# Block-causal attention and two FFN layers: the low words' shift on ScalarE, their scaling within VectorE's product, and two early weight halves instead of four

## The chip, the cores and the metric

The kernel runs on one core of one Trainium2 chip. The metric is the device time of one execution in microseconds (us). Before the change three runs took 1007.52, 1007.89 and 1008.43 us; their median is 1007.89 us.

Five engines work in parallel, each on its own queue in order: TensorE (PE in the profile; its weight loads are PEld), VectorE (DVE), ScalarE (ACT), GpSimd (POOL) and SyncE (SP, which here only issues transfers).

## The reference, cut to what matters

The input is q, k, v of shape (4, 8, 576, 64) in float32 and two pairs of weights of 512x2048 and 2048x512.

```python
# block-causal attention: a query sees the keys of its own block of 64 and of earlier blocks
scores = q @ k.T / 8, masked;  attn = softmax(scores);  attn_out = attn @ v
x = attn_out as 2304 tokens x 512
h = x @ w_in;   x = relu(h)**2 @ w_out          # first FFN layer  ("layer 0")
h = x @ w2_in;  y = (h * cos(h)) @ w2_out       # second FFN layer ("layer 1")
```

## The kernel before, in words

**Attention.** Batch and head give 32 attentions, taken two at a time: 16 pairs, 0 to 15. For each pair there are nine blocks of 64 queries. PE makes the scores of a block (`add_scores`), DVE their maximum, ACT the exponentials with their sums; GpSimd scales the probabilities by the reciprocal of the sums (L431), PE transposes them (L452), ACT and DVE split them into a high and a low part (L457, L460), GpSimd splits the values in the same way (L486, L492), PE multiplies (L517), ACT moves one half across the partitions (L528) and DVE adds and writes the result into `xall` (L531, "join"). The order of all this on each engine is not written out: a planner (`Plan`, L52 on) puts every step into an order by walking through the program with an assumed cost for each step. Among steps that could start at the same moment it takes the one with the lowest rank, and the rank is the step's number in the program plus the entry of its kind in the table `RANK`.

**Weights.** The weights of both layers come as float64. A "half" (class `Half`) is one 128x512 chunk of `w_in` or of `w_out`, 512 KB, loaded into a `raw` tile (four buffers), in which each weight is a low and a high 32-bit word. Its steps turn the two words into two float32 tiles, a high part and a remainder, that PE then multiplies: on DVE `shift` (L205), `mask` (L212), `join` (L223), `sign` (L235), `power` (L241) and `low` (L265); on ACT `rebias` (L218), `fraction` (L229) and `high` (L256, a copy). `low` multiplies the scaled low words by each weight's power of two. Layer 0 has 32 halves and layer 1 another 32.

**Early halves.** Four halves of layer 0 are converted by the planner inside attention (`add_half`), not before the first score step of the last pair (the key `late`); their `high` runs on GpSimd (L259). Their raw words are loaded early.

**Layers.** Each layer goes over blocks of up to 512 tokens, and each block over 16 chunks of 128 hidden features, which gives one *step* per chunk. In a step PE makes `hidden` of this chunk (12 matmuls, L619) and `output` of the chunk three steps back (12 matmuls, L683); in between, ACT and DVE turn the hidden values into a high part (L631) and a low part `gs` (L634). At each step `convert` is called as often as the table `PACE` says: twice per step in block 0, which is how the other 28 halves of layer 0 are made while block 0 runs. One call of `convert` finishes the half that the call before began and begins the next. In layer 0's last block the halves of layer 1 follow, 1.75 calls per step and 0.75 in the block after it. At the end of a block the next block's tokens are split as well (class `Cut`, L315 on ACT and L318 on DVE), into one set of `xs` tiles.

**PSUM.** Attention uses eight banks: six handed round by the planner (`ps0` to `ps5`) and two for the widest block. The layers use the same eight, `h0` to `h3` on the places of `ps0` to `ps3`. So the first `hidden` (into `h1`) can't be written until the last reader of `ps1` in attention is done.

Of the kernel before, what the change touches and what calls it, by code (L numbers as in the profile page):

```python
# [24 lines left out]


RANK = {
    "load": -388.7,
    "k scale": -506.7,
    "scores": 0.2,  # L30
    "maximum": -16.0,
    "exponential": 485.3,
    "guard": -148.0,
    "invert": -12.1,
    "scale": -145.6,
    "turn": 13.1,
    "turned high": -90.7,
    "turned low": -1.1,
    "value load": -78.8,
    "value high": -109.4,  # L40
    "value low": 28.0,
    "weighted": 21.6,
    "move": 1000,
    "join": 34.2,
    "keep": 67.5,
    "add": 125.4,
    "zeros": -32.1,
    "weights": 181.2,
    "cut": 1000000.0,
}  # L50

# [1 line left out]
class Plan:  # L53
# [12 lines left out]
        self.steps, self.wrote, self.readers = [], {}, {}  # L66
        self.held, self.taken = {}, {}

    def add(self, engine, cost, at, emit, reads=(), writes=(), holds=0, frees=None):
        n, after, (kind, rank) = len(self.steps), set(), at  # L70
        rank += RANK[kind]
        for key in reads:
            after.add(self.wrote.get(key))
            self.readers.setdefault(key, []).append(n)
        for key in writes:
            after.add(self.wrote.get(key))
            after.update(self.readers.pop(key, ()))
            self.wrote[key] = n
        self.steps.append((engine, cost, rank, emit, after - {None, n}, holds, frees))
        return n  # L80

    def emit(self):
        waits = [len(step[4]) for step in self.steps]
        follow = [[] for _ in self.steps]
        for n, step in enumerate(self.steps):
            for m in step[4]:
                follow[m].append(n)
        able, clock = {}, {}
        start = [0.0] * len(self.steps)
        for n, step in enumerate(self.steps):  # L90
            clock[step[0]] = 0.0
            able.setdefault(step[0], [])
            if not waits[n]:
                able[step[0]].append(n)
        free = [(0.0, b) for b in range(len(self.banks))]
        held = self.held
        for _ in self.steps:
            best = None
            for engine, mine in able.items():
                times = {}  # L100
                for n in mine:
                    holds = self.steps[n][5]
                    if holds <= len(free):
                        times[n] = max(start[n], clock[engine], free[holds - 1][0] if holds else 0.0)
                if times:
                    t = min(times.values())
                    n = min((n for n in times if times[n] <= t), key=lambda n: (self.steps[n][2], n))
                    if best is None or t < best[0]:
                        best = (t, n)
            t, n = best  # L110
            engine, cost, _, emit, _, holds, frees = self.steps[n]
            able[engine].remove(n)
            clock[engine] = t + cost
            if holds:
                self.taken[n] = [free.pop(0)[1] for _ in range(holds)]
                held[n] = [self.banks[b] for b in self.taken[n]]
            key = n if holds else frees
            emit(*(held[key] if key is not None else []))
            if frees is not None:
                free = sorted(free + [(t + cost + 0.37, b) for b in self.taken[frees]])  # L120
            for m in follow[n]:
                other = self.steps[m][0]
                lag = self.SIGNAL.get((engine, other), 0.06 if engine == other else 0.15)
# [7 lines left out]
def tile_block_causal_attention__then__two_ffn(  # L131
# [38 lines left out]
    nc.vector.memset(new_bias, -7.0 * 2.0**30)  # L170

    WARM = 15
    EARLY = 4
    NA = 5
    w_a = ctx.enter_context(tc.tile_pool(name="w_a", bufs=NA))
    xs_p = ctx.enter_context(tc.tile_pool(name="xs", bufs=1))
# [16 lines left out]
    class Half:  # L193
# [8 lines left out]
            nc.sync.dma_start(out=self.raw, in_=packed[self.key[0]][self.key[1], self.h])  # L202

        def shift(self):
            nc.vector.tensor_scalar(  # L205
                out=self.low_word, in0=self.low_word, scalar1=9, scalar2=None,
                op0=ALU.logical_shift_right,
            )

        def mask(self):  # L210
# [11 lines left out]
        def join(self):  # L222
            nc.vector.scalar_tensor_tensor(  # L223
                out=self.low_word, in0=self.high_word, scalar=23, in1=self.low_word,
                op0=ALU.logical_shift_left, op1=ALU.bitwise_or,
            )

        def fraction(self):
            nc.scalar.activation(  # L229
                out=self.low_word.bitcast(F32), in_=self.low_word.bitcast(U32), func=AF.Copy,  # L230
                scale=2.0**-43,
            )

        def sign(self):
# [20 lines left out]
        def high(self):  # L255
            nc.scalar.copy(out=self.room()[:, 0], in_=self.bits.bitcast(F32))  # L256

        def high_beside(self):
            nc.gpsimd.tensor_scalar(  # L259
                out=self.room()[:, 0], in0=self.bits.bitcast(F32), scalar1=1.0, scalar2=0.0,  # L260
                op0=ALU.mult, op1=ALU.add,
            )

        def low(self):
            nc.vector.tensor_tensor(  # L265
                out=self.room()[:, 1], in0=self.low_word.bitcast(F32),
                in1=self.high_word.bitcast(F32), op=ALU.mult,
            )

    later = []  # L270

    def flush():
        while later:
            later.pop()()

    def convert():

        old = new = None
        flush()
        if begun:  # L280
            (layer, c), h = begun[0].key, begun[0].h
            if layer == 1 and c >= freed[h]:
# [3 lines left out]
        if loaded:  # L286
            new = loaded.pop(0)
            begun.append(new)
            new.shift()
        if old:  # L290
            old.power()
            old.high()
        if new:
            new.mask()
            new.rebias()
        if old:
            old.low()
        if new:
            new.join()
            later.append(new.fraction)  # L300
        if loads:
            loaded.append(Half(*loads.pop()))
            loaded[-1].load()
# [21 lines left out]
    def attention():  # L325
        with ExitStack() as actx:
# [224 lines left out]
            def add_half(n):  # L551
                x = Half(*loads.pop())
                raw, high, bits = f"raw{n % 4}", f"high{n % 4}", f"bits{n % 2}"
                rank = ("weights", n)
                late = f"S{NPAIR - 1}.0"
                plan.add("D", 2.0, rank, x.load, writes=[raw, high])
                plan.add("V", 0.34, rank, x.shift, [late], [raw])
                plan.add("V", 0.34, rank, x.mask, [high, late], [bits])
                plan.add("A", 0.61, rank, x.rebias, writes=[bits])
                plan.add("V", 0.6, rank, x.join, [high], [raw])  # L560
                plan.add("A", 0.52, rank, x.fraction, writes=[raw])
                plan.add("V", 0.6, rank, x.sign, [high], [bits])
                plan.add("V", 0.34, rank, x.power, [bits], [high])
                plan.add("G", 0.67, rank, x.high_beside, [bits])
                plan.add("V", 0.6, rank, x.low, [raw, high])

            make_identity(nc, ident)

# [31 lines left out]
    def layers():  # L600
# [112 lines left out]
                t0 += n  # L713
        last = max(i for i, b in enumerate(blocks) if b[0] == 0)
        steps = [(i, c) for i in range(len(blocks)) for c in range(KF)]
        PACE = {0: 2, last: 1.75, last + 1: 0.75}
        owed = 0.0
        gss = {}
        xs = first
# [1 line left out]
        for step in range(len(steps) + LAG):  # L721
# [10 lines left out]
            for a, z in zip_longest(begin, [None] + end):  # L732
                for f in (a, z):
                    if f:
                        f()
                flush()
# [68 lines left out]
```

## Time and profile before

| | us |
|---|---|
| median of three runs | 1007.89 |
| the profiled execution | 1008.09 |
| its span, first to last instruction | 1006.3 |
| PE busy | 981.6 (98%) |
| DVE busy | 638.2 (63%) |
| ACT busy | 585.1 (58%) |
| POOL busy | 142.1 (14%) |

Attention takes the first 188 us or so, block 0 of layer 0 the time up to about 287 us, and the rest of both layers the time up to the end. The profiled execution lasts 1.8 us longer than its span. A busy PE means only that matmuls were in flight, since they are pipelined; whether PE was held up is read from the start times of equal groups of matmuls. A share of busy time over the whole span says little here, as the stages have different limits: each stage is to be read by itself.

### The profile page before, as it was taken

The page shows a single profiled execution, that of the slowest core. Times are in us where ns is not written, and L with a number is a line of the kernel's source. Part 1 is how long each engine was busy: PE and PEld are TensorE (multiplying, and loading weights), DVE is VectorE, ACT ScalarE, POOL GpSimd, SP SyncE. Part 2 cuts the span into 40 slices and gives each one's busy share as a digit, 9 for nine tenths or more (in the row PEclk, how much of TensorE's full clock was granted, in tenths as well). Part 3 has the DMA queues.
Part 4 walks back from the last instruction along what each step waited for, and adds up shares of the span by engine and source line. Part 5 has one row for each costly group of instructions (what it writes and reads, how often), then busy time and mean ns, then how long its engine had stood idle before and what let it go on. Part 6 is the DMA issues. An engine that isn't in the chain of part 4 may idle for free.

```text
span 1006.3 us, 13883 instructions
## 1 busy us (share of the span) xinstructions
PE 981.6 (98%) x4895; PEld 826.7 (82%) x4895; DVE 638.2 (63%) x1292; ACT 585.1 (58%) x1194; POOL 142.1 (14%) x258
## 2 busy tenths in 40 slices
PE   9999999699989999999999999999999999999998
PEld 7888887577768889988888888888888888899997
DVE  6998899999941111121168998976646555656554
ACT  7999999688863344443367886644334333434433
POOL 6777767400000000000000000000000000000000
PEclk9999999899989999999999999999999999999999
DMA  6433331254410000000013442000000100100000
GB/s 212 150 117 127 98 110 50 95 175 170 168 63 1 1 1 1 2 1 1 1 63 112 170 137 84 21 1 32 11 1 1 42 1 1 43 1 1 32 1 31
DMA packets 18805, 58.56 MB, mean 58 GB/s; under 512 B 1968, under 2 KB 2096, under 8 KB 18736
## 3 DMA queue, kind: packets, MB, share of 16 engines
q1 hardware_dynamic: 18736, 57.68, 16.5%
q8 instruction: 38, 0.62, 0.2%
q14 instruction: 31, 0.25, 0.1%
HBM read 52.95 MB, written 4.72 MB: 57 GB/s over the span
## 4 chain that ended last, share of the span: by engine, by line
PE 75%; DVE 18%; ACT 3%; issue 2%; POOL 1%; DVEq 0%; ACTq 0%; POOLq 0%
PE acc L683 32%; PE h L619 31%; PE ps L374 4%; PE ps L517 3%; DVE bits L235 3%; DVE w L265 3%; PE ps L452 3%; DVE raw L223 3%; DVE raw L205 2%; DVE raw L241 2%; DVE gs L634 1%; DVE PTl L460 1%; PE wide L374 1%; DVE nmax L386 1%; POOL P L431 1%
## 5 line engine op out<-in xcount | busy, mean ns | idle before, releaser
L619 PE MATMUL h<-xs,w 128*128 128x512 f32 (+2 forms) x1920 | 425.7, 371 | 8.3 <-DVE xall L531 5.3
L619 PEld LDWEIGHTS h<-xs,w 128*128 128x128 f32 x1920 | 347.7, 190 | 65.4 <-ACT raw L229 5.4
L683 PE MATMUL acc<-gs,w 128*128 128x512 f32 (+1 forms) x960 | 214.3, 370 | 5.6 <-DVE gs L634 5.6
L683 PE MATMUL acc<-w,gs 128*128 128x512 f32 x864 | 209.8, 391 | 0.4 <-ACT xall L696 0.4
L683 PEld LDWEIGHTS acc<-gs,w 128*128 128x128 f32 x960 | 167.9, 189 | 40.4 <-DVE gs L634 10.7
L634 DVE TENSOR_TENSOR gs<-g,gs 128x512 fp32r<-128x512 f32 (+2 forms) x160 | 101.3, 634 | 146.2 <-ACT gs L631 146.1
L683 PEld LDWEIGHTS acc<-w,gs 128*128 128x128 f32 x864 | 161.6, 188 | 32.9 <-ACT xall L696 0.8
L631 ACT CAST gs<-g 128x512 fp32r<-128x512 f32 (+2 forms) x160 | 92.3, 577 | 153.0 <-DVE g L666 96.0
L652 DVE SCALAR_TENSOR_TENSOR g<-turns,h 128x512 f32<-128x512 int32 (+1 forms) x80 | 50.7, 634 | 122.2 <-ACT turns L649 121.6
L374 PE MATMUL ps<-kB,qB 128*128 128x64 f32 (+7 forms) x256 | 84.1, 419 | 0.9 <-ACT P L391 0.9
L641 ACT ACTIVATE g<-h 128x512 f32<-128x512 f32 (+1 forms) x80 | 43.9, 549 | 69.8 <-PE h L619 69.0
L649 ACT ACTIVATE turns<-h 128x512 int32<-128x512 f32 (+1 forms) x80 | 44.2, 552 | 68.6 <-PE h L619 68.5
L431 POOL TENSOR_SCALAR P<-P,rinv 128x64 f32<-128x64 f32 (+2 forms) x144 | 78.3, 562 | 34.0 <-DVE rinv L422 33.9
L663 ACT ACTIVATE g<-g,half_pi 128x512 f32<-128x512 f32 (+1 forms) x80 | 54.6, 682 | 37.6 <-DVE g L657 37.6
L391 ACT ACTIVATE P<-ps,nmax 128x64 f32<-128x64 f32 (+7 forms) x128 | 64.6, 506 | 8.9 <-DVE nmax L386 7.2
L452 PEld LDWEIGHTS ps<-ident,P 128*128 128x128 f32 (+1 forms) x400 | 47.4, 140 | 25.3 <-issue 12.5
L460 DVE TENSOR_TENSOR PTl<-ps,PTh 128x512 fp32r<-128x512 f32 x96 | 63.6, 682 | 1.1 <-ACT PTh L457 0.5
L386 DVE TENSOR_REDUCE nmax<-ps 128x1 f32<-128x64 f32 (+7 forms) x128 | 57.2, 448 | 7.0 <-PE ps L374 6.2
L452 PE MATMUL ps<-ident,P 128*128 128x128 f32 (+1 forms) x400 | 59.4, 275 | 2.0 <-POOL P L431 1.9
L457 ACT CAST PTh<-ps 128x512 fp32r<-128x512 f32 (+1 forms) x112 | 58.2, 544 | 5.4 <-PE ps L452 3.7
L517 PE MATMUL ps<-PTh,vhl 128*128 128x320 f32 (+3 forms) x224 | 58.0, 296 | 1.4 <-POOL vhl L492 1.0
L218 ACT ACTIVATE bits<-bits,new_bias 128x512 int32<-128x512 int32 x64 | 46.4, 725 | 20.0 <-DVE bits L212 20.0
(50 smaller groups left out, 938.0 us busy)
## 6 DMA issues: line engine op xcount, KB each, us to landing
raw<-in_w_dram SPq DMA_DIRECT2D x64, 512.0 KB, 3.6
qB<-in_qd_dram SPq DMA_DIRECT2D x15, 576.0 KB, 4.0
v_raw<-in_vp_dram SPq DMA_DIRECT2D x16, 320.0 KB, 2.9
kB<-in_kT_dram SPq DMA_DIRECT2D x16, 288.0 KB, 2.8
out_dram<-o SPq DMA_DIRECT2D x8, 512.0 KB, 3.4
out_dram<-o SPq DMA_DIRECT2D x2, 256.0 KB, 2.9
qB<-in_qd_dram SPq DMA_DIRECT2D x1, 384.0 KB, 4.5
qB<-in_qd_dram SPq DMA_DIRECT2D x1, 192.0 KB, 2.9
```

Source lines behind the costliest of these rows:

```text
L374: nc.tensor.matmul(bank[:, 0:w] if one else wide[:, x, 0:w], lhsT=qB[r][:, i].rearrange("p e d -> p (e d)"), rhs=kB[r][:, x * w : (x + 1) ...
L386: nc.vector.tensor_reduce(out=nmax[i], in_=held(), axis=AX.X if one else AX.XY, op=ALU.max, negate=True)
L391: nc.scalar.activation(out=mine if one else mine.rearrange("p (x w) -> p x w", x=2), in_=held(), func=AF.Exp, bias=nmax[i], scale=1.0, acc ...
L431: nc.gpsimd.tensor_scalar(out=mine, in0=mine, scalar1=inverse[:, i - i0 : i - i0 + 1], scalar2=1.0, op0=ALU.mult, op1=ALU.mult,)
L452: nc.tensor.transpose(bank[0:keys, n * 128 : (n + 1) * 128], P[r][:, o : o + keys], ident)
L457: nc.scalar.copy(out=PT[0][0:keys, at], in_=plan.held[s][0][0:keys, 0:w])
L460: nc.vector.tensor_tensor(out=PT[1][:, at] if keys == 128 else PT[0][keys:128, at], in0=bank[0:keys, 0:w], in1=PT[0][0:keys, at].bitcast(F32),
L517: nc.tensor.matmul(bank[:, (a - i0) * D : w], lhsT=vhl[:, j, e].rearrange("p x d -> p (x d)"), rhs=pt[x][:, s0 : s0 + i1 - a, e, :], start ...
L619: nc.tensor.matmul(h, lhsT=w[:, a, kk * 128 : (kk + 1) * 128], rhs=xs[kk].parts[:, x], start=(m == 0), stop=(m == 3 * KD - 1),)
L631: nc.scalar.copy(out=gs[:, 0], in_=g)
L634: nc.vector.tensor_tensor(out=gs[:, 1], in0=g, in1=gs[:, 0].bitcast(F32), op=ALU.subtract)
L683: nc.tensor.matmul(dst, lhsT=lhsT, rhs=rhs, start=(c == 0 and m == 0), stop=(c == KF - 1 and m == 2),)
```

## The change

Per half: `shift` becomes an ACT instruction (a copy from unsigned to unsigned integers with a scale that stands for the shift by 9), so it leaves DVE; `fraction` is gone from ACT, and its scale 2^-43 is put into DVE's `low`, which becomes a SCALAR_TENSOR_TENSOR with two multiplications on the same tiles. In `convert`, `mask` now stands ahead of `power`, which puts `power` directly in front of `low`, and the deferred call of `fraction` (`later`, `flush`) goes.

In attention two halves are converted instead of four, without the key that kept them late, with `high` on ACT and nothing on GpSimd; the planner now takes each of their DVE steps as also holding GpSimd for its cost (`beside`). The table of ranks is new throughout. In layer 0's last block `convert` is called twice per step, not 1.75 times. 30 halves of layer 0 are left for the layers in place of 28.

```diff
 RANK = {
-    "value low": 28.0,
+    "value low": -58.0,
...
-    "weights": 181.2,
+    "weights": 343.4,
...
+            if beside:
+                t = max(t, clock[beside])
+                clock[beside] = t + cost
...
-    EARLY = 4
+    EARLY = 2
...
         def shift(self):
-            nc.vector.tensor_scalar(
-                out=self.low_word, in0=self.low_word, scalar1=9, scalar2=None,
-                op0=ALU.logical_shift_right,
+            nc.scalar.activation(
+                out=self.low_word.bitcast(U32), in_=self.low_word.bitcast(U32), func=AF.Copy,
+                scale=2.0**-9 * (1.0 - 2.0**-23),
             )
...
-        def fraction(self):
-            nc.scalar.activation(
-                out=self.low_word.bitcast(F32), in_=self.low_word.bitcast(U32), func=AF.Copy,
-                scale=2.0**-43,
-            )
...
-        def high_beside(self):
-            nc.gpsimd.tensor_scalar(
-                out=self.room()[:, 0], in0=self.bits.bitcast(F32), scalar1=1.0, scalar2=0.0,
-                op0=ALU.mult, op1=ALU.add,
-            )
-
         def low(self):
-            nc.vector.tensor_tensor(
-                out=self.room()[:, 1], in0=self.low_word.bitcast(F32),
-                in1=self.high_word.bitcast(F32), op=ALU.mult,
-            )
+            nc.vector.scalar_tensor_tensor(
+                out=self.room()[:, 1], in0=self.low_word.bitcast(U32), scalar=2.0**-43,
+                in1=self.high_word.bitcast(F32), op0=ALU.mult, op1=ALU.mult,
+            )
...
             new.shift()
+            new.mask()
         if old:
+            old.high()
             old.power()
-            old.high()
         if new:
-            new.mask()
             new.rebias()
         if old:
             old.low()
         if new:
             new.join()
-            later.append(new.fraction)
...
-                late = f"S{NPAIR - 1}.0"
                 plan.add("D", 2.0, rank, x.load, writes=[raw, high])
-                plan.add("V", 0.34, rank, x.shift, [late], [raw])
-                plan.add("V", 0.34, rank, x.mask, [high, late], [bits])
...
+                both = dict(beside="G")
+                plan.add("A", 0.56, rank, x.shift, writes=[raw])
+                plan.add("V", 0.45, rank, x.mask, [high], [bits], **both)
...
+                plan.add("A", 0.52, rank, x.high, [bits])
+                plan.add("V", 0.75, rank, x.low, [raw, high], **both)
...
-        PACE = {0: 2, last: 1.75, last + 1: 0.75}
+        PACE = {0: 2, last: 2, last + 1: 0.75}
```

Three places show how the order moves. The line numbers after the change differ: `mask` is L216, `join` L227, `sign` L233, `power` L239, `low` L257 on DVE; `shift` is L209, `rebias` L222, `high` L254 on ACT; the join into `xall` is L515, `gs` L617.

DVE at the end of attention, before: the last pair's four joins into `xall` (L531; three of them are in this piece, the fourth follows) and between them the steps of the second, third and fourth early half.

```order
L531 TENSOR_TENSOR xall_60<-ps5_88,half0_117 64x256
L235 SCALAR_TENSOR_TENSOR bits_2128<-raw_460,bits_2128 128x512
L205 TENSOR_SCALAR raw_481<-raw_481 128x512
L241 TENSOR_SCALAR raw_460<-bits_2128 128x512
L212 TENSOR_SCALAR bits_2153<-raw_481 128x512
L265 TENSOR_TENSOR w0_2150<-raw_460 128x512
L223 SCALAR_TENSOR_TENSOR raw_481<-raw_481 128x512
L235 SCALAR_TENSOR_TENSOR bits_2153<-raw_481,bits_2153 128x512
L531 TENSOR_TENSOR xall_60<-ps1_84,half0_117 64x320
L241 TENSOR_SCALAR raw_481<-bits_2153 128x512
L531 TENSOR_TENSOR xall_60<-ps0_83,half1_118 64x256
L265 TENSOR_TENSOR w1_2161<-raw_481 128x512
```

The same place after: the last transposed part, the four joins in a row, and then the first half that `convert` makes (the third of layer 0).

```order
L444 TENSOR_TENSOR PTh_100<-ps0_83,PTh_100 64x128
L515 TENSOR_TENSOR xall_60<-ps3_86,half0_117 64x256
L515 TENSOR_TENSOR xall_60<-ps2_85,half1_118 64x256
L515 TENSOR_TENSOR xall_60<-ps5_88,half0_117 64x320
L515 TENSOR_TENSOR xall_60<-ps4_87,half1_118 64x320
L216 TENSOR_SCALAR bits_2176<-raw_459 128x512
L227 SCALAR_TENSOR_TENSOR raw_459<-raw_459 128x512
L233 SCALAR_TENSOR_TENSOR bits_2176<-raw_459,bits_2176 128x512
L216 TENSOR_SCALAR bits_2184<-raw_478 128x512
L239 TENSOR_SCALAR raw_459<-bits_2176 128x512
L257 SCALAR_TENSOR_TENSOR w0_2186<-raw_459 128x512
```

No weight step stands between the joins any more. The join that reads `ps1`, whose bank the first `hidden` needs, was among the last and now belongs to the pair before; the last pair's joins read `ps3`, `ps2`, `ps5` and `ps4`.

DVE in a step of block 0, before: the low part `gs`, then one call of `convert` (`sign`, `shift`, `power`, `mask`, `low`, `join`); a second one follows.

```order
L634 TENSOR_TENSOR gs<-g,gs 128x512
L235 SCALAR_TENSOR_TENSOR bits<-raw,bits 128x512
L205 TENSOR_SCALAR raw<-raw 128x512
L241 TENSOR_SCALAR raw<-bits 128x512
L212 TENSOR_SCALAR bits<-raw 128x512
L265 TENSOR_TENSOR w_2288<-raw 128x512
L223 SCALAR_TENSOR_TENSOR raw<-raw 128x512
```

The same after (with the buffers' numbers):

```order
L617 TENSOR_TENSOR gs_2207<-g_2206,gs_2207 128x512
L233 SCALAR_TENSOR_TENSOR bits_2267<-raw_2233,bits_2267 128x512
L216 TENSOR_SCALAR bits_2297<-raw_2263 128x512
L239 TENSOR_SCALAR raw_2233<-bits_2267 128x512
L257 SCALAR_TENSOR_TENSOR w1_2299<-raw_2233 128x512
L227 SCALAR_TENSOR_TENSOR raw_2263<-raw_2263 128x512
```

One instruction of six is gone, and `low` (L257) now follows directly on `power` (L239), whose result it reads; before, `mask` (L212) of the next half stood between them.

DVE in the middle of attention, before: pair 1's four joins with one split of the first 512 tokens (L318) among them.

```order
L531 TENSOR_TENSOR xall_60<-ps2_85,half0_117 64x256
L531 TENSOR_TENSOR xall_60<-ps0_83,half1_118 64x256
L318 TENSOR_TENSOR xs0_363<-xall_60,xs0_363 128x512
L531 TENSOR_TENSOR xall_60<-ps5_88,half0_117 64x320
L531 TENSOR_TENSOR xall_60<-ps1_84,half1_118 64x320
L386 TENSOR_REDUCE nmax3_105<-ps2_85 128x1
L460 TENSOR_TENSOR PTl_101<-ps4_87,PTh_100 128x512
```

The same place after: two steps of the first early half (`mask` L216 and `join` L227) stand among the joins.

```order
L515 TENSOR_TENSOR xall_60<-ps3_86,half0_117 64x256
L216 TENSOR_SCALAR bits_447<-raw_331 128x512
L515 TENSOR_TENSOR xall_60<-ps5_88,half1_118 64x256
L227 SCALAR_TENSOR_TENSOR raw_331<-raw_331 128x512
L515 TENSOR_TENSOR xall_60<-ps0_83,half0_117 64x320
L370 TENSOR_REDUCE nmax3_105<-ps3_86 128x1
L444 TENSOR_TENSOR PTl_101<-ps4_87,PTh_100 128x512
```

The ten DVE steps of the two early halves now lie spread over six pairs (1 to 6), where GpSimd is also at work; the splits stay in this part of attention, some rows later.

## Rows read from the trace of the kernel before

**Rows 1.** Busy time by stretch: us, then PE, PEld, DVE, ACT, POOL, clock, DMA share, GB/s

```profile
20.00:160.00 140.00, 139.70 (x904) 117.58 (x904) 127.87 (x298) 129.85 (x374) 106.06 (x191) 1.00 0.36 123
...
206.00:281.00 75.00, 69.57 (x292) 53.62 (x291) 75.00 (x157) 63.74 (x109) 0.00 (x0) 1.00 0.49 169
284.00:296.00 12.00, 8.98 (x26) 6.91 (x27) 4.35 (x7) 7.46 (x14) 0.00 (x0) 0.72 0.13 44
296.00:600.00 304.00, 304.00 (x1523) 259.56 (x1522) 115.62 (x223) 155.24 (x279) 0.00 (x0) 1.00 0.11 39
```

**Rows 2.** The chain that ended last, pairs 0 and 9: start us, us, what

```profile
21.38 2.80 PE ps L517 x22
...
120.57 2.80 PE ps L517 x22
```

**Rows 3.** PE's waits from 188 us to the end: total us, times, longest us

```profile
PE acc L683 <- DVE gs L634: 5.6, 12, 0.5
PE h L619 <- DVE xall L531: 5.3, 1, 5.3
PE h L619 <- ACT xs L315: 3.0, 1, 3.0
```

**Rows 4.** Timeline of PE: start us, us, engine line op, count, idle before and releaser

```profile
184.66 0.39 PE L517 MATMUL ps<-PTh,vhl 128*128 128x256 f32 x1 [0.69 <-POOL vhl L492]
...
193.49 13.19 PE L619 MATMUL h<-xs,w 128*128 128x512 f32 x48 [5.29 <-DVE xall L531]
...
287.02 5.79 PE L619 MATMUL h<-xs,w 128*128 128x512 f32 x12 [3.04 <-ACT xs L315]
...
295.72 2.88 PE L619 MATMUL h<-xs,w 128*128 128x512 f32 x12
...
301.16 2.88 PE L619 MATMUL h<-xs,w 128*128 128x512 f32 x12
```

**Rows 5.** Timeline of DVE at the end of attention: an early mask, a join

```profile
166.85 0.90 DVE L212 TENSOR_SCALAR bits<-raw 128x512 int32<-128x512 int32 x1
...
192.87 0.47 DVE L531 TENSOR_TENSOR xall<-ps,half 64x320 f32<-64x320 f32 x1
```

**Rows 6.** Timeline of DVE in block 0: one `gs`, one `convert`, the last full step

```profile
205.70 0.69 DVE L634 TENSOR_TENSOR gs<-g,gs 128x512 fp32r<-128x512 f32 x1
206.30 0.69 DVE L235 SCALAR_TENSOR_TENSOR bits<-raw,bits 128x512 int32<-128x512 int32 x1
...
206.90 0.42 DVE L205 TENSOR_SCALAR raw<-raw 128x512 int32<-128x512 int32 x1
...
207.91 0.69 DVE L265 TENSOR_TENSOR w<-raw 128x512 fp32r<-128x512 f32 x1
...
208.51 0.69 DVE L223 SCALAR_TENSOR_TENSOR raw<-raw 128x512 int32<-128x512 int32 x1
...
280.45 0.70 DVE L634 TENSOR_TENSOR gs<-g,gs 128x512 fp32r<-128x512 f32 x1
```

**Rows 7.** Timeline of ACT in attention: exponentials of 512 keys, pairs 14 and 15

```profile
163.06 0.69 ACT L391 ACTIVATE P<-ps,nmax 128x512 f32<-128x512 f32 x1
...
175.66 0.69 ACT L391 ACTIVATE P<-ps,nmax 128x512 f32<-128x512 f32 x1
```

**Rows 8.** Timeline of POOL in attention: scaling alone and at the end, split, early high parts

```profile
57.83 0.75 POOL L431 TENSOR_SCALAR P<-P,rinv 128x576 f32<-128x576 f32 x1
...
177.38 4.89 POOL L431 TENSOR_SCALAR P<-P,rinv 128x320 f32<-128x320 f32 x5 [0.66 <-DVE rinv L422]
...
183.06 1.55 POOL L492 TENSOR_TENSOR vhl<-v_raw,vhl 128x640 fp32r<-128x640 f32 x1
...
190.21 3.96 POOL L259 TENSOR_SCALAR w<-bits 128x512 fp32r<-128x512 f32 x2 [2.82 <-DVE bits L235]
```

**Rows 9.** Timeline of DVE in layer 1: two instructions, the second reads the first's result

```profile
612.49 0.68 DVE L652 SCALAR_TENSOR_TENSOR g<-turns,g 128x512 f32<-128x512 int32 x1
613.20 0.43 DVE L657 TENSOR_SCALAR g<-g 128x512 int32<-128x512 int32 x1
```

More of the change, by code (lines that the diff above doesn't have):

```diff
@@ L27 @@
 RANK = {
[L28 to L40, printed above, removed]
-    "value low": 28.0,
[L42 to L47, printed above, removed]
-    "weights": 181.2,
+    "load": -507.9,
+    "k scale": 108.1,
+    "scores": 0.9,
+    "maximum": -16.6,
+    "exponential": 83.3,
+    "guard": -193.8,
+    "invert": -90.7,
+    "scale": -191.6,
+    "turn": 13.3,
+    "turned high": -150.0,
+    "turned low": -2.0,
+    "value load": -324.3,
+    "value high": -388.7,
+    "value low": -58.0,
+    "weighted": 22.1,
+    "move": 220.4,
+    "join": 289.3,
+    "keep": -7.8,
+    "add": 169.5,
+    "zeros": -205.7,
+    "weights": 343.4,
     "cut": 1000000.0,
@@ L67, in __init__, with add @@
         self.held, self.taken = {}, {}
-    def add(self, engine, cost, at, emit, reads=(), writes=(), holds=0, frees=None):
+    def add(self, engine, cost, at, emit, reads=(), writes=(), holds=0, frees=None, beside=None):
         n, after, (kind, rank) = len(self.steps), set(), at
@@ L78, in add @@
             self.wrote[key] = n
-        self.steps.append((engine, cost, rank, emit, after - {None, n}, holds, frees))
+        self.steps.append((engine, cost, rank, emit, after - {None, n}, holds, frees, beside))
         return n
@@ L110, in emit @@
             t, n = best
-            engine, cost, _, emit, _, holds, frees = self.steps[n]
+            engine, cost, _, emit, _, holds, frees, beside = self.steps[n]
             able[engine].remove(n)
+            if beside:
+                t = max(t, clock[beside])
+                clock[beside] = t + cost
             clock[engine] = t + cost
@@ L256, in high, with low @@
             nc.scalar.copy(out=self.room()[:, 0], in_=self.bits.bitcast(F32))
-        def high_beside(self):
-            nc.gpsimd.tensor_scalar(
-                out=self.room()[:, 0], in0=self.bits.bitcast(F32), scalar1=1.0, scalar2=0.0,
-                op0=ALU.mult, op1=ALU.add,
-            )
-        def low(self):
-            nc.vector.tensor_tensor(
-                out=self.room()[:, 1], in0=self.low_word.bitcast(F32),
-                in1=self.high_word.bitcast(F32), op=ALU.mult,
-            )
[L270 to L274, printed above, removed]
+        def low(self):
+            nc.vector.scalar_tensor_tensor(
+                out=self.room()[:, 1], in0=self.low_word.bitcast(U32), scalar=2.0**-43,
+                in1=self.high_word.bitcast(F32), op0=ALU.mult, op1=ALU.mult,
+            )
     def convert():
         old = new = None
-        flush()
         if begun:
@@ L554, in add_half @@
                 rank = ("weights", n)
-                late = f"S{NPAIR - 1}.0"
                 plan.add("D", 2.0, rank, x.load, writes=[raw, high])
-                plan.add("V", 0.34, rank, x.shift, [late], [raw])
-                plan.add("V", 0.34, rank, x.mask, [high, late], [bits])
[L559 to L565, printed above, removed]
+                both = dict(beside="G")
+                plan.add("A", 0.56, rank, x.shift, writes=[raw])
+                plan.add("V", 0.45, rank, x.mask, [high], [bits], **both)
+                plan.add("A", 0.63, rank, x.rebias, writes=[bits])
+                plan.add("V", 0.75, rank, x.join, [high], [raw], **both)
+                plan.add("V", 0.75, rank, x.sign, [high], [bits], **both)
+                plan.add("V", 0.45, rank, x.power, [bits], [high], **both)
+                plan.add("A", 0.52, rank, x.high, [bits])
+                plan.add("V", 0.75, rank, x.low, [raw, high], **both)
             make_identity(nc, ident)
@@ L735, in layers @@
                         f()
-                flush()
             if step < len(steps) and c == KF - 1 and i + 1 < len(blocks):
```

## The prediction, on record before the run

> **What bounds the kernel now.** I read the busy times by stretch first, as PE's 98% over the span is an average over stages with different limits. In the middle of attention PE is busy for 139.7 of 140 us, DVE for 127.9 and GpSimd for 106 [rows 1]. The chain of waits shows that PE really is the bound there: the large group of value products starts at 21.38 us for pair 0 and at 120.57 us for pair 9 [rows 2], so a pair takes 11.02 us, and the chain has nothing but PE in between. In block 0 it is DVE: 75.0 of 75.0 us busy [rows 1]. From 296 us on PE has no gap [rows 1], and its steps are 301.16 - 295.72 = 5.44 us apart [rows 4].
>
> PE's waits are then the list of what can be won: 12 waits on `gs` in block 0, one of 5.3 us on a join as the layers start, one of 3.0 us on the split between blocks 0 and 1 [rows 3]. After the second and third the granted clock is low: 0.72 in the mean of 284 to 296 us [rows 1], and the 12 matmuls from 287.02 us take 5.79 us against 2.88 later [rows 4], so they ran at 1.2 GHz, not 2.4.
>
> So I follow one clock: when DVE reaches `gs` of its step 2 (205.70 us), of its step 14 (280.45 us), and when PE starts step 17 (295.72 us) [rows 4, 6]. Whatever is won by then stays, since PE has no gap behind it.
>
> **Term 1, the start of the layers.** Four early halves stand in the last pairs on DVE. The exponential over 512 keys comes 12.60 us after that of the pair before [rows 7], where the pace is 11.02: 1.6 us late. With the weight steps gone I put it at 163.06 + 11.02 = 174.1 us. It is over by 174.9; the guard on GpSimd and the reciprocal on DVE, behind one join, end at 175.9. Of the five scalings three are done by 176.5, and the last two (0.75 us each, as one alone takes) end at 178.0, against 177.38 + 4.89 = 182.3 before [rows 8]. Behind them come the values' split (its high part about as long as a scaling, its low part 1.55 us [rows 8]) and the first product: 180.4 to 181, against 184.66 [rows 4]. The products last from there to 193.49 - 5.29 = 188.2, so 3.5 us; they would end at T = 184.3.
>
> Then PE waited 5.3 us for the join that reads `ps1`, since DVE had weight steps in front of it and reached it at 192.87 us [rows 3, 5]. After the change `ps1`'s last reader belongs to the pair before, and the first two chunks of `w_in` have long been converted: PE goes on at T. What is late next is the third chunk, which `convert` makes: the last move and join end at T + 1.1 = 185.4; mask and join with the wait for ACT's rebias take 1.35; three calls at the new price (2.60, below) bring DVE to its step 2 at 185.4 + 1.35 + 7.8 = 194.55 us. PE has hidden steps 0 and 1 (half of 5.44, 2.72 us each) and waits about a microsecond for the next ones. Against 205.70 this is 11.15 us earlier. Bounds for T: 183.5 (every tie falls well) to 188.2 (the products end as before).
>
> **Term 2, the pace in block 0.** From start to start a call costs 0.60 (sign) + 1.01 (shift, power and mask, from 206.90 to 207.91, a third each) + 0.60 (low) + 0.60 (join) = 2.81 us, and `gs` 0.60 [rows 6]; twice 2.81 and 0.60 are the 6.23 us of a step: (280.45 - 205.70) / 12. Shift goes. But `low` now reads the result of the instruction just ahead of it. The nearest row is L657 behind L652: 0.71 us from start to start, where the same 0.68 us instruction lets an independent one start after 0.60 [rows 6, 9], so 0.11 us more. A call becomes 2.81 - 0.33 + 0.12 = 2.60 us, a step 0.60 + 5.20 = 5.80, still above PE's 5.44, so DVE stays the bound, now through the weights of the next chunk and not through `gs`. Twelve steps win 12 x 0.43 = 5.1 us: step 14 at 194.55 + 69.7 = 264.3 us. The two more halves for the layers are in this: the calls are there at every step anyway, and step 14 now has two full ones. `low` with its extra scale I take at the price of L235, a SCALAR_TENSOR_TENSOR of the same shape: 0.69 us, as the product before [rows 6]. ACT gets a shift for a fraction, both strided copies, and was busy for 63.7 of 75 us [rows 1]: 5.3 us per step, which fits into 5.8. If shift has to wait for its transfer, rebias, `high` and the activations wait behind it on ACT; the transfers ran at 169 GB/s with half the DMA engines' time free [rows 1], and a half per 2.9 us is 181 GB/s, so I put no wait there.
>
> The Trainium skill (VectorE: DVE Perf Modes, section on the DRAIN that cannot be avoided) says that eight copies take the same time with a semaphore after each as with one after the last, so a wait between DVE instructions is free. By it a call would be 2.48 us and the whole 2.8 us better; rows 9 disagree by 0.11 us, and the measurement decides. It is the lower end of this term.
>
> **Term 3, from block 0 to block 1.** DVE's step 14 is followed by step 15 at 264.3 + 5.8 = 270.1 us. ACT ends rebias of step 14 some 0.75 us earlier, does the three activations in front of the split (1.65 us) and ends the first split at 271.3. PE, through with step 15 at 269.2, waits 2.1 us for it and 0.5 for the low part, and starts step 17 at 277.3 us: 13.0 us after DVE's step 14, against 295.72 - 280.45 = 15.3 before. The 2.3 us are the slow clock less what the fuller step 14 costs. A wait of 3.0 us was followed by 1.2 GHz; in block 0, with 12 waits of half a microsecond, the clock stayed at 1.00 [rows 1, 3]. Two waits of 2.1 and 0.5 us with matmuls between lie between these; I take the faster level, and 3.3 us more as the upper end.
>
> **Term 4, the middle of attention.** The ten DVE steps of the early halves (about 5.2 us) now stand in six PE-bound pairs. DVE has 140 - 127.9 = 12.1 us to spare over 12.7 pairs, 0.95 per pair [rows 1]; they need 0.87, and the splits stand there too. A step beside GpSimd is slower: mask took 0.90 us in attention; the 0.42 us of shift, power and mask alike is block 0's [rows 5, 6]. Bounds: 0 (all in gaps) to 5 us (each step late by 0.5). I take 1.5 us lost, nearer to the lower end as both engines have gaps.
>
> **Term 5, the rest.** With two calls in layer 0's last block a step of DVE is 5.8 us against PE's 5.44 for some ten steps, 3.6 us of lag. The last block's `gs` is needed a step and a half after it is made, so this lag is hidden; what it costs if not is the wait at the next split, up to 3 us. I take 0.
>
> **Sum.** 295.72 - 277.3 = 18.4 us won, 1.5 lost: 16.9 us. The profiled execution took 1008.09 us, span and the 1.8 us around it, so 991.2; it was 0.2 us above the median, so I predict 991.0 us.
>
> **The rivals.** (a) *GpSimd is held in attention.* Were all ten steps and GpSimd's delayed scalings felt by PE, attention would lose 5 to 10 us and the time be 995 to 1000 us. For it: the five scalings took 4.89 us beside weight steps and would take 3.2 alone, two early copies 3.96 us for 1.4 [rows 8]. Against: GpSimd is idle for a quarter of that stretch [rows 1]. The Trainium skill (SBUF — State Buffer, who interferes with whom) calls the shared ports an exclusive lock that a DVE instruction with two SBUF inputs or in a two-port mode takes for its whole length; the 0.90 us mask and the 3.96 us agree that one waits for the other. (b) *The same, and slower than before.* A hold of GpSimd delays the scaling of a pair, its transposes and PE by the same time. The worst seen, 3.96 - 0.75 = 3.2 us for one copy, is 2.5 us too long; ten of these on the path are 25 us, and the time 1015 us. It decides from 1.84 us per step on. Against it: that copy stood beside a row of weight steps without a break, which attention's middle does not have. (c) *DVE's step hardly falls*, because shift on ACT or the double product is slower than the rows say; then only terms 1 and 3 remain: about 996 us. (d) *All goes well*: free wait, T = 183.5, nothing lost in attention: 18.4 + 2.8 + 0.8 = 22.0 us won, 986 us.
>
> **How the numbers follow.** Forecast within 3 us: 0.50; (d) 0.17; (a) with slow-clock or split costs 0.20; (c) 0.07; (b) 0.03; 0.03 for an order of attention that loses all of it by another way. The range 985 to 1000 us takes in T = 188.2 or (a) or the slow clock with one more loss. A measurement of this kernel can tell 0.2%, about 2 us, from no change: all but (b) and the last case are faster; 0.94 faster, 0.02 the same, 0.04 slower.
>
> **What would show it.** Right: no PE wait on a join as the layers start, first `hidden` near 184 to 186 us; DVE's `gs` 5.8 us apart in block 0 with PE waiting on the weights' `low`; step 17 near 277 us. Wrong: `gs` 6.2 us apart, value products more than 11.1 us apart in pairs 1 to 6, a wait of PE at layer 1's start.

## The result and the profile after

The changed kernel took 997.73 us in the median of four runs (996.26 to 1000.02), against 1008.16 us: ratio 0.9895, interval 0.9871 to 0.9919. It is 10.4 us faster where 16.9 were forecast: inside the range, 6.7 us above the point.

The profiled execution was the slowest of the four: 1000.02 us, span 998.2 us. It answers the prediction's clock row by row. First PE's waits, which answer to [rows 3], here over the whole span (total us, times, longest us):

```profile
PE h L602 <- ACT xs L299: 3.1, 2, 2.7
PE ps L358 <- DMA qB<-in_qd_dram: 2.0, 1, 2.0
...
PE h L602 <- ACT w L254: 0.9, 1, 0.9
```

The wait on a join is gone, and so are the twelve on `gs`. The split between blocks 0 and 1 still costs 2.7 us, and 2.0 us on a transfer of q are new. The timeline of PE shows the last product of pairs 0, 13 and 15 (of before first, then of after), then the layers' start, and the split between blocks 0 and 1:

```profile
23.97 0.22 PE L517 MATMUL ps<-PTh,vhl 128*128 128x64 f32 x1
...
167.23 0.22 PE L517 MATMUL ps<-PTh,vhl 128*128 128x64 f32 x1
...
187.98 0.22 PE L517 MATMUL ps<-PTh,vhl 128*128 128x64 f32 x1
```

```profile
26.37 0.22 PE L501 MATMUL ps<-PTh,vhl 128*128 128x64 f32 x1
...
174.48 0.22 PE L501 MATMUL ps<-PTh,vhl 128*128 128x64 f32 x1
...
190.85 0.22 PE L501 MATMUL ps<-PTh,vhl 128*128 128x64 f32 x1
190.90 5.47 PE L602 MATMUL h<-xs,w 128*128 128x512 f32 x23
...
278.84 0.51 PE L602 MATMUL h<-xs,w 128*128 128x512 f32 x1 [2.73 <-ACT xs L299]
279.56 4.03 PE L602 MATMUL h<-xs,w 128*128 128x512 f32 x11 [0.22 <-DVE xs L302]
...
286.53 2.88 PE L602 MATMUL h<-xs,w 128*128 128x512 f32 x12
```

Pair 0 ends 2.40 us later than before. From there to the end of pair 13 before took 143.26 us (13 x 11.02), after 148.11. From pair 13 to pair 15 it was 20.75 us, now it is 16.37. PE goes straight from the last product to the first `hidden`. At the split 11 matmuls take 4.03 us; at full speed 12 take 2.88. The granted clock is 0.89 in the mean of the stretch behind (us, PE, PEld, DVE, ACT, POOL, clock, DMA share, GB/s):

```profile
281.00:296.00 15.00, 15.00 (x61) 12.24 (x60) 4.87 (x9) 7.01 (x12) 0.00 (x0) 0.89 0.10 35
```

The timeline of DVE in block 0, the `gs` of step 2, and then one `gs` to the next (answers to [rows 6]):

```profile
201.43 0.69 DVE L617 TENSOR_TENSOR gs<-g,gs 128x512 fp32r<-128x512 f32 x1
...
265.49 0.69 DVE L617 TENSOR_TENSOR gs<-g,gs 128x512 fp32r<-128x512 f32 x1
266.09 0.69 DVE L233 SCALAR_TENSOR_TENSOR bits<-raw,bits 128x512 int32<-128x512 int32 x1
266.69 0.42 DVE L216 TENSOR_SCALAR bits<-raw 128x512 int32<-128x512 int32 x1
267.03 0.42 DVE L239 TENSOR_SCALAR raw<-bits 128x512 int32<-128x512 int32 x1
267.49 0.69 DVE L257 SCALAR_TENSOR_TENSOR w<-raw 128x512 fp32r<-128x512 uint32 x1
...
271.30 0.69 DVE L617 TENSOR_TENSOR gs<-g,gs 128x512 fp32r<-128x512 f32 x1
```

This step is 5.81 us, and `low` starts 0.46 us after `power`, which starts 0.34 after `mask`. 271.30 is step 14.

GpSimd's low part of the values in attention:

```profile
84.16 1.54 POOL L476 TENSOR_TENSOR vhl<-v_raw,vhl 128x640 fp32r<-128x640 f32 x1
```

DVE in attention, an early step beside it, and two splits in a row:

```profile
84.52 1.47 DVE L239 TENSOR_SCALAR raw<-bits 128x512 int32<-128x512 int32 x1
85.91 0.48 DVE L370 TENSOR_REDUCE nmax<-ps 128x1 f32<-128x320 f32 x1
...
105.41 2.04 DVE L302 TENSOR_TENSOR xs<-xall,xs 128x512 fp32r<-128x512 f32 x2
107.48 0.69 DVE L444 TENSOR_TENSOR PTl<-ps,PTh 128x512 fp32r<-128x512 f32 x1
```

`power`, 0.42 us in block 0, takes 1.47, and the maximum that the next exponential needs stands behind it and starts 1.39 us after it: this pair (6) takes 12.44 us, 1.42 more than 11.02. The splits of the first 512 tokens stood one per pair before; now two stand together (in this place and at 117.35 us), and each of these two pairs is over 1 us too long (12.04 and 12.17).

### The profile page after: what moved, and what is told of

Same layout as the page of the kernel before. It is cut to its first block, busy times and chain, and to the rows that moved or that the text cites. A ratio compares the mean times of both kernels' runs of the same rounds, so it can differ in the third digit from the quotient of the medians.

```text
span 998.2 us, 13639 instructions
## 1 busy us (share of the span) xinstructions
PE 983.4 (99%) x4895; PEld 822.8 (82%) x4895; DVE 622.8 (62%) x1228; ACT 583.8 (58%) x1198; POOL 135.8 (14%) x254
## 4 chain that ended last, share of the span: by engine, by line
PE 78%; DVE 17%; ACT 3%; issue 1%; DMA 1%; POOL 0%; POOLq 0%; SPq 0%; DVEq 0%; ACTq 0%
PE acc L666 32%; PE h L602 31%; PE ps L358 6%; PE ps L501 4%; PE ps L436 4%; DVE w L257 3%; DVE bits L233 3%; DVE raw L227 3%; DVE raw L239 2%; DVE bits L216 2%; DVE gs L617 1%; PE wide L358 1%; DVE nmax L370 1%; ACT bits L222 1%; DMA qB<-in_qd_dram 1%
## 5 line engine op out<-in xcount | busy, mean ns | idle before, releaser
L602 PEld LDWEIGHTS h<-xs,w 128*128 128x128 f32 x1920 | 343.2, 188 | 68.4 <-DVE w L257 5.9
L666 PE MATMUL acc<-gs,w 128*128 128x512 f32 (+1 forms) x960 | 210.6, 368 | 0.0
L617 DVE TENSOR_TENSOR gs<-g,gs 128x512 fp32r<-128x512 f32 (+2 forms) x160 | 101.2, 633 | 142.2 <-ACT gs L614 142.1
L415 POOL TENSOR_SCALAR P<-P,rinv 128x64 f32<-128x64 f32 (+2 forms) x144 | 75.7, 543 | 27.8 <-DVE rinv L406 26.3
L257 DVE SCALAR_TENSOR_TENSOR w<-raw 128x512 fp32r<-128x512 uint32 x64 | 45.0, 702 | 11.2 <-PE h L602 6.7
```

The lines of the kernel that those rows point to most:

```text
L257: nc.vector.scalar_tensor_tensor(out=self.room()[:, 1], in0=self.low_word.bitcast(U32), scalar=2.0**-43, in1=self.high_word.bitcast(F32), ...
L415: nc.gpsimd.tensor_scalar(out=mine, in0=mine, scalar1=inverse[:, i - i0 : i - i0 + 1], scalar2=1.0, op0=ALU.mult, op1=ALU.mult,)
L602: nc.tensor.matmul(h, lhsT=w[:, a, kk * 128 : (kk + 1) * 128], rhs=xs[kk].parts[:, x], start=(m == 0), stop=(m == 3 * KD - 1),)
L617: nc.vector.tensor_tensor(out=gs[:, 1], in0=g, in1=gs[:, 0].bitcast(F32), op=ALU.subtract)
L666: nc.tensor.matmul(dst, lhsT=lhsT, rhs=rhs, start=(c == 0 and m == 0), stop=(c == KF - 1 and m == 2),)
```

## The experiments

All compare with the kernel before, whose median was 1007.65 to 1008.16 us throughout. Kernels 1 to 4, 5 to 8 and 9 to 12 each ran together. An interval is some 1 to 2 us wide to either side, so smaller differences between kernels are read from the traces.

| run | median us | ratio (interval) | pairs 0 to 13, us | `gs` step, us |
|---|---|---|---|---|
| changed kernel | 997.73 | 0.9895 (0.9871-0.9919) | 148.11 | 5.82 |
| e1 conversion only | 998.97 | 0.9915 (0.9902-0.9929) | 143.82 | 5.82 |
| e2 no early half | 998.64 | 0.9911 (0.9897-0.9924) | 143.99 | 5.82 |
| e3 splits spread | 996.18 | 0.9887 (0.9873-0.9900) | 146.33 | 5.82 |
| e4 one step per pair | 994.73 | 0.9871 (0.9858-0.9885) | 144.66 | 5.82 |
| e5 no `beside` | 998.85 | 0.9915 (0.9901-0.9930) | 149.89 | 5.82 |
| e6 `mask` between | 999.38 | 0.9922 (0.9907-0.9937) | 148.09 | 5.88 |
| e7 split first | 993.39 | 0.9868 (0.9850-0.9887) | 148.09 | 5.82 |
| e8 e4 + e6 + e7 | 992.87 | 0.9859 (0.9839-0.9880) | 144.61 | 5.86 |
| e9 `join` between | 993.27 | 0.9855 (0.9838-0.9871) | 148.15 | 5.62 |
| e10 e4 + e7 + e9 | 986.51 | 0.9786 (0.9773-0.9799) | 144.65 | 5.60 |
| e11 e10, 1.75 calls | 986.12 | 0.9783 (0.9769-0.9796) | 144.65 | 5.61 |
| e12 plan only | 1010.24 | 1.0025 (1.0017-1.0034) | 148.10 | 6.25 |

The last two columns are from the trace of each: last product of pair 0 to that of pair 13, and DVE's `gs` from step 2 to step 14 over 12.

**e1 and e12, one half of the change each.** e1 is the kernel before with the change's hunks in `Half` and `convert` alone. e12 is the changed kernel with the old instructions and their order in `convert`:

```diff
-            new.shift()
-            new.mask()
+            new.shift_dve()
...
-            old.low()
+            old.low_plain()
...
+            later.append(new.fraction)
```

> The kernel before with the new conversion alone (shift on ScalarE, scale folded into low, mask ahead of power): four early halves, their key, the old table of ranks and 1.75 calls stay. If the conversion's price is what the prediction's term 2 says, VectorE's step in block 0 falls from 6.23 to 5.80 us, attention keeps 11.02 us per pair, and the time is 1008.2 - 5 - about 1 (less in the last pairs) = 1002 us. Rival: the gain is all in the new order of attention and the conversion gives nothing: 1008 us.

> The changed kernel with the old conversion in the layers (shift on VectorE, the scale in fraction on ScalarE, six VectorE instructions per call); attention, the two early halves and the table stay. VectorE's step in block 0 is then 6.23 us again: 12 x 0.41 and three calls at the start lose 5.5 us, 1003 us. So the new plan alone would give about 5 us of the 10, and the conversion alone gave 8.7: the two together fall short of their sum by 3.5 us. Rival (the plan alone gives nothing, as attention's loss takes what its end wins): 1007 us.

e1 gained 8.7 us, more than expected; e12 lost 2.4 us, where it was to gain 5. The step was as expected in both. What differs is the splits (PE, e1 first):

```profile
279.69 0.49 PE L611 MATMUL h<-xs,w 128*128 128x512 f32 x1 [1.70 <-ACT xs L308]
280.42 2.82 PE L611 MATMUL h<-xs,w 128*128 128x512 f32 x11 [0.23 <-DVE xs L311]
...
285.81 2.88 PE L611 MATMUL h<-xs,w 128*128 128x512 f32 x12
```

```profile
283.35 5.79 PE L628 MATMUL h<-xs,w 128*128 128x512 f32 x12 [3.88 <-ACT xs L325]
...
598.14 5.58 PE L628 MATMUL h<-xs,w 128*128 128x512 f32 x12 [4.20 <-ACT xs L325]
```

With 28 halves for the layers e1's DVE has half a step less in front of the split: PE waits 1.7 us and the clock stays up (granted 1.00 from 280 to 295 us). In e12 PE waits 3.9 us there, and 4.2 us more at the first split of layer 1, each followed by 12 matmuls at half speed. The second wait is term 5's: with 6.25 us per step, two calls per step put the layer's last block behind; the kernel before, with about the same step and 1.75 calls, has no wait there (e12 with 1.75 calls was not run). The new conversion makes those two calls bearable, so the halves of the change are no two independent gains.

**e2 to e5, what slows attention.** e2 and e5 change one line each:

```diff
-    EARLY = 2
+    EARLY = 0
```

```diff
-                both = dict(beside="G")
+                both = dict()
```

e3 and e4 tie steps to the second of a pair's four joins, so that the planner can't place them earlier; `x_of(p)` names that join of pair p. e3 does it for the splits alone (with 8 in place of 11), e4 for the weight steps too:

```diff
+            def x_of(p):
+                return f"x{p // KD}.{p % KD}.1.0"
...
+                in_pair = lambda k: x_of(1 + 5 * n + k)
...
-                both = dict(beside="G")
+                both = dict()
...
-                plan.add("V", 0.45, rank, x.mask, [high], [bits], **both)
+                plan.add("V", 0.45, rank, x.mask, [high, in_pair(0)], [bits], **both)
...
-                plan.add("V", 0.6, ("cut", kk), x.low, [f"xs{kk}"])
+                plan.add("V", 0.6, ("cut", kk), x.low, [f"xs{kk}", x_of(11 + kk)])
```

> The changed kernel with no early half at all, so attention has no weight step; VectorE's four splits then stand one per pair, in pairs 1 to 4. If the weight steps and the doubled splits are what slows attention, all pairs run at 11.02 us and attention ends about 4.9 us earlier than in the changed kernel; the layers then have two calls more to make before they get going, 5.2 us, so the time is about 998 us. Rival: the new order of attention is slow by itself: pairs 2 to 9 still average 11.5 us, and the time is 1003 us.

> The changed kernel with the low splits of the first 512 tokens one per pair (pairs 8 to 11) in place of two in pair 7 and two in pair 8. Theory of the slot (VectorE has about 1.1 us free at one place of a pair, and only what goes beyond it delays PE): the 2.2 us that pairs 8 and 9 lose go away, 995.5 us. Rival (each VectorE instruction that holds GpSimd delays the pair, wherever it stands): no change, 997.7 us.

> The changed kernel with the ten VectorE steps of the two early halves one per pair, behind the second join of pairs 1 to 10, and the four low splits one per pair in pairs 11 to 14; the planner's entry on GpSimd is dropped for them. Theory of the slot: every pair runs at 11.02 us, attention ends 4.9 us earlier and the time is 993 us. Rival (holding GpSimd is what costs): the ten steps still cost their 2.9 us, only the doubled splits' 2.2 us may go: 995.5 to 997.7 us.

> The changed kernel with the planner's entry on GpSimd (beside) left out. The planner then puts the ten weight steps into pairs 1 to 3 and the four splits into pairs 3 and 4. Theory of the slot (1.1 us free per pair on VectorE, what goes beyond it delays PE): by the durations in the changed kernel the steps of pairs 1 to 4 exceed it by about 1.9, 2.0, 1.6 and 2.0 us, 7.5 us, where the changed kernel's exceed it by 3.8; so 3.7 us slower than the changed kernel, 1001.4 us. Rival (holding GpSimd is what costs): as many holds as before, no difference, 997.7 us.

The changed kernel's 13 pairs exceed 13 x 11.02 = 143.26 us by 4.85. Without weight steps 0.73 is left (e2), so that much is the new table's own; what in it does this was not tried. Spreading the splits alone gives 1.78 back (e3), one step or split per pair 3.45 (e4; the time is 994.73 us, where 993 was expected). In e4 the ten steps still run beside GpSimd and are as stretched as before, two of them:

```profile
79.25 0.97 DVE L257 SCALAR_TENSOR_TENSOR w<-raw 128x512 fp32r<-128x512 uint32 x1
...
123.84 0.81 DVE L239 TENSOR_SCALAR raw<-bits 128x512 int32<-128x512 int32 x1
```

All ten together take 8.7 us there, 8.3 in the changed kernel (5.8 at block 0's durations), and attention is 0.67 us longer than with none, where the rival asked for 2.9 us. GpSimd is held there too: its scaling of k, 0.67 us alone, takes up to 1.11. So the theory of the slot holds: a pair has one gap of about 1 us on DVE, behind its second join, and a step put there costs little, stretched or not. The gap, in a pair of the changed kernel without side work (the third join, and the idle time before it):

```profile
141.43 0.48 DVE L515 TENSOR_TENSOR xall<-ps,half 64x320 f32<-64x320 f32 x1 [1.03 <-ACT half L512]
```

The rival, that holding GpSimd costs as much wherever the step stands, is refuted. The changed kernel's dearest step, the `power` at 84.52 us, stands outside the gap, between two maxima. e5 went the way expected, by less: 1.8 us more in attention, where 3.7 were forecast; in the time it is 1.1 us, and the intervals of the two kernels overlap. By the trace pairs 2 to 5 take 6.35 us more than 4 x 11.02, where 7.5 were expected.

**e6 and e9, the price of a dependent neighbour.** e6 puts `mask` back between `power` and `low`; e9 leaves it in front and puts `join` there. The diff is e9's:

```diff
             new.mask()
         if old:
             old.high()
             old.power()
         if new:
             new.rebias()
+            new.join()
         if old:
             old.low()
-        if new:
-            new.join()
```

> The changed kernel with mask put back between power and low in convert, so that low no longer stands directly behind the instruction whose result it reads. If this dependence is what makes low start 0.46 us after power and not 0.34, a call costs 2.49 us in place of 2.61, VectorE's step in block 0 falls from 5.82 to 5.58 us, and some 27 calls win 3.2 us: 994.5 us. Rival 1 (the second multiplication makes low dearer, not the dependence): no change, 997.7 us. Rival 2 (mask later means rebias later on ScalarE, and sign waits for it): step above 5.82 us, slower than 997.7 us.

> The changed kernel with the next half's join put between power and low (sign, mask, power, join, low), so that no VectorE instruction of a call directly follows the one whose result it reads. In the run before, mask between power and low freed low but put power directly behind sign. If the 0.12 us belongs to any two dependent neighbours, a call costs 2.49 us, the step in block 0 falls from 5.82 to 5.58 us, and the time is 997.7 - 3.1 = 994.6 us. Rival (join, now 0.6 us earlier, waits for ScalarE's shift, which ended 0.8 us ahead of it): step 5.7 us or above, 996 us or more.

DVE in block 0 of e6, then of e9:

```profile
205.23 0.68 DVE L233 SCALAR_TENSOR_TENSOR bits<-raw,bits 128x512 int32<-128x512 int32 x1
205.95 0.43 DVE L239 TENSOR_SCALAR raw<-bits 128x512 int32<-128x512 int32 x1
206.29 0.42 DVE L216 TENSOR_SCALAR bits<-raw 128x512 int32<-128x512 int32 x1
206.62 0.69 DVE L257 SCALAR_TENSOR_TENSOR w<-raw 128x512 fp32r<-128x512 uint32 x1
```

```profile
204.45 0.69 DVE L233 SCALAR_TENSOR_TENSOR bits<-raw,bits 128x512 int32<-128x512 int32 x1
205.05 0.42 DVE L216 TENSOR_SCALAR bits<-raw 128x512 int32<-128x512 int32 x1
205.38 0.42 DVE L239 TENSOR_SCALAR raw<-bits 128x512 int32<-128x512 int32 x1
205.72 0.69 DVE L227 SCALAR_TENSOR_TENSOR raw<-raw 128x512 int32<-128x512 int32 x1
206.32 0.69 DVE L257 SCALAR_TENSOR_TENSOR w<-raw 128x512 fp32r<-128x512 uint32 x1
206.92 0.69 DVE L616 TENSOR_TENSOR gs<-g,gs 128x512 fp32r<-128x512 f32 x1
```

In e6 `low` starts 0.33 us after its neighbour, but now `power` reads the result of `sign` just ahead and starts 0.72 after it, not 0.60: the 0.12 us only moved, and e6's expected gain was an oversight in the chain of reads. (Its step is longer still, as `sign` waits for a later `rebias` at times.) In e9 no neighbour depends on the one before: a call is 2.47 us here and the step 5.62, 0.04 above what was expected, as `join` at times waits for ScalarE's shift. The time is 4.5 us less. By the profile 2.4 of it are twelve shorter steps, and 1.8 come after step 17 (709.9 us from there to the end, 711.7 in the changed kernel), where PE no longer waits at layer 1's start: the shorter step leaves no lag in layer 0's last block. The Trainium skill (VectorE: DVE Perf Modes, The DRAIN you can't avoid) says of eight copies that a semaphore after each costs nothing extra; for two neighbours of which one reads the other's result these runs show 0.12 us, and the measurement decides.

**e7, e8, e10 and e11, the split, and the parts together.** e7 moves the split of the next block's tokens ahead of the activations of the step before:

```diff
+            if step < len(steps) and c == KF - 1 and i + 1 < len(blocks):
+                xs = [Cut(*blocks[i + 1][1:], kk) for kk in range(KD)]
...
             for a, z in zip_longest(begin, [None] + end):
```

> The changed kernel with the split of the next block's tokens put ahead of the activations of the step before it. ScalarE's three activations (1.8 us) then no longer stand in front of the split: PE's wait between blocks 0 and 1 falls from 2.7 to about 0.9 us. If the clock then stays at 2.4 GHz, 1.8 us of wait and about 1.9 us of slow matmuls go: 994 us. Rival 1 (the clock falls after the shorter wait as well): 996 us. Rival 2 (the activations, now 2.2 us later, are waited for a step and a half later): what is won comes back, 997 us.

> The changed kernel with three edits at once: one weight step or split per pair, mask between power and low, and the split ahead of the activations. If the three work at different places, the time is 997.7 - 3.0 (measured) - 3.2 - 3.7 = 988 us. Rival (a shorter step on VectorE brings block 0 near PE's 5.44 us, so the gains do not add): 991 us.

> The changed kernel with one weight step or split per pair, the split ahead of the activations, and join between power and low. If the three add: 997.7 - 3.0 - 4.3 (both measured) - 3.1 = 987.3 us. Rival (PE's wait at the split grows again as block 0 gets shorter on VectorE alone, and the clock falls): 989.5 us.

> The kernel of the run before this one, with 1.75 calls per step in layer 0's last block again in place of 2. From step 17 to the end the changed kernel took 711.7 us of its profile, with 1.75 calls the kernel with the new conversion alone took 710.9 us. If that is the pace: 0.9 us less, 986.4 us. Rival (the difference comes from elsewhere): 987.3 us.

The split in e7:

```profile
274.23 0.50 PE L602 MATMUL h<-xs,w 128*128 128x512 f32 x1 [0.92 <-ACT xs L299]
275.05 2.79 PE L602 MATMUL h<-xs,w 128*128 128x512 f32 x11 [0.32 <-DVE xs L302]
```

A wait of 0.9 us, the clock at 2.4 GHz behind it (granted 1.00 from 275 to 290 us), and 4.3 us won: by the profile 3.3 up to step 17 and 1.1 behind it. e8 carries e6's order, which wins nothing, and so wins less than the expected sum (992.87 us where 988 was expected); its profile waits 1.3 us and has 11 matmuls in 4.07 us. e10 puts together what worked and takes 986.51 us, 21 us less than before and 11 less than the changed kernel; the three gains (3.0, 4.3 and 4.5 us) nearly add. PE's waits on `hidden` in e10 are at most 1.0 us, and those at the split 0.2:

```profile
PE h L605 <- ACT w L254: 1.0, 1, 1.0
...
PE h L605 <- DVE w L257: 0.5, 1, 0.5
...
PE h L605 <- DVE xs L301: 0.2, 1, 0.2
PE h L605 <- ACT xs L298: 0.2, 1, 0.2
```

e11 differs from e10 by less than the intervals, and in both the part from step 17 to the end takes 709.9 us: with the shorter step, 1.75 calls win nothing.

## Why the prediction was right in direction and too large in its gain

The mechanism of its gains held (terms 1 and 2). Its reading of attention did not (term 4), and two more costs were taken too small (terms 3 and 5). Two of its own signs of being wrong came true: pairs 2 to 6 take 11.22 to 12.44 us, above 11.1, and PE waits at layer 1's start. The time stayed inside the range because the range allowed for the slow clock with one more loss, and about this came. The profiled execution was forecast at 991.2 us and took 1000.02. The 8.8 us, in the prediction's terms:

- **Start of attention, not in the sum: 2.4 us.** The second part of the first q landed 5.8 us after its issue and PE waited 2.0 us. The same six transfers are issued in the same order as before. In the twelve experiments this wait was between none and 1.8 us, and pair 0 ended at 23.4 to 26.3 us: it varies from run to run. It is probably why this execution is 2.3 us above its median of 997.73; the other three were not profiled.
- **Term 4, the middle of attention: 1.5 us forecast, 4.85 measured.** This is the step that failed, at the top of its bounds (0 to 5). It pooled DVE's free time, 0.95 us per pair, and let splits and steps share it. The runs show one gap per pair; two splits in it, or a step outside it, push the next pair (pairs 6, 8 and 9 alone lose 3.6 us). The splits' move, which the order showed, I had taken as harmless: e3 puts 1.8 us on it. Rival (a) named the right time, 995 to 1000 us, and the wrong cause. GpSimd is not what PE waits for (e4). In pair 6 it is the other direction that matters: beside GpSimd's 1.54 us low part, which started 0.36 us earlier and kept its length, `power` took 1.47 us. The Trainium skill (SBUF — State Buffer, Who interferes with whom) says that the order of issue decides who blocks; the rows at 84.16 and 84.52 us agree.
- **Term 1, the end of attention: 0.4 us better than forecast.** From the last product of pair 13 to the end of pair 15's (T) 17.1 us were forecast and 16.6 came; PE goes on at once, and DVE's step 2 follows T by 10.4 us (10.25 forecast).
- **Term 2, the pace in block 0: right.** 5.82 us per step against 5.80, 0.2 us over twelve steps, and the extra 0.12 us of `low` to the hundredth. This extra was also an offer that I did not see: another order of the same instructions (e9) takes it away.
- **Term 3, the split: 2.2 us too low.** Step 17 comes 15.2 us after DVE's step 14, where 13.0 were forecast. About 0.5 us of it are the wait, 2.7 us where 2.1 were forecast (ACT's three activations in front of the split take 1.8 us, not 1.65), and 1.7 the slow matmuls behind it (11 in 4.03 us); I took the faster level for waits of 2.1 and 0.5 us, with no row between 0.5 and 3.0 to go by. e7 shows both prices together: with 0.9 us of wait, step 17 comes 11.9 us after step 14.
- **Term 5, the rest: 1.1 us instead of 0.** From step 17 to the end it is 711.7 us, before 710.6. All of it falls on the first split of layer 1, 0.6 us of it as waits of PE (0.38 and 0.23 us). e12 shows what it grows to with a longer step: 4.2 us and slow matmuls.

Terms 1 and 2 alone were right to half a microsecond; the gains were sound, and the costs were each taken near their cheaper end.

## What to carry to other kernels

Free time of an engine beside a bound one is not a pool: look for where in the period the gap stands and how long it is, and put one piece of side work into each gap. Within a row of instructions on VectorE, put something independent between a result and its reader. And a wait of TensorE of two or three microseconds costs twice, once as the wait and once as the slow matmuls behind it; shorten it by what stands in front of the awaited work on its engine.

## What the runs showed of the hardware

- An instruction on VectorE that reads the result of the one directly ahead starts 0.12 us later than an independent one: 0.46 against 0.34 us behind a 0.42 us instruction, 0.72 against 0.60 behind a 0.69 us one.
- TensorE after a wait at the split between blocks 0 and 1: 0.9 and 1.7 us (e7, e1) were followed by 2.4 GHz, 11 matmuls in 2.79 and 2.82 us. 1.3 us (e8) and all from 2.0 us up were followed by the slow level for some or all of the next 12 (4.03 to 4.37 us for 11, 4.67 to 5.79 for 12). The granted clock of the 15 us behind was 1.00 in e7 and e1, 0.89 in the changed kernel, e8 and e9, and 0.79 in the kernel before and e12. Why 1.7 us once did less harm than 1.3 stays open.
- VectorE beside GpSimd: the same `power` takes 0.42 us alone, 0.55 and 0.81 in e4's slots beside scalings, and 1.47 beside the two-input low part of 1.54 us. The other way round, in e5 a `sign` that started 0.22 us ahead of the low part kept its 0.68 us, and the low part took 1.85.
